# The second MLP's first layer in seven block products in place of eight

## The chip, the cores and the metric

The kernel runs on one core of a Trainium2 chip. The metric is the device time of one execution in microseconds (us); before the change the median of three runs is 594.81 us (594.66 to 596.38). The engines are named as the profile names them: PE (TensorE, the matrix multiplier), DVE (VectorE), ACT (ScalarE), POOL (GpSimd) and SP (which only issues DMAs here).

## The reference

A linear recurrence over 4 sequences of 768 tokens and 8 heads makes 3072 rows of 256 features, and two MLPs follow, each 256 to 2048 to 256:

```python
x = attn_out.transpose(0, 2, 1, 3).reshape(3072, 256)
x = softplus(x @ w_in1) @ w_out1
h = x @ w_in2                      # 256 -> 2048: what is changed
g = h * (1.0 / (1.0 + np.exp(-1.702 * h)))
out = g @ w_out2
```

## The kernel before, in words

Tokens are worked through in 6 chunks of 512 columns (`NC`, `TB`); features lie on the partitions. An MLP on one chunk is 16 tiles (`NF`), one for each 128 of the 2048 inner features; tile t runs from 0 to 191, 0 to 95 the first MLP and 96 to 191 the second. The recurrence is interleaved with the first MLP's first chunks. Chunk 5 (tiles 80 to 95) is the first MLP's last, chunk 6 (tiles 96 to 111) the second MLP's first.

An fp32 operand is held as a high half rounded to the matmul's format (fp32r) and a low half, the difference; one product is then three matmuls (high by high, high by low, low by high). For each tile, `g1` (L386) makes h with 6 matmuls (two contraction halves of 128 features, three each) in one of three PSUM banks `ps_h`. ACT applies the activation (L593) and rounds it to gh (`rnd`, L411), DVE makes the low half gl (`low`, L416), and two tiles later `g2` (L393) adds the tile into the output with 6 matmuls, three for each 128 output features j. `finish` (L421) copies a finished chunk's output from PSUM on ACT or DVE, and for the second MLP sends it to HBM from one of two buffers tagged "e". The MLPs' weights come as 64-bit floats in 16 units each, of 128 x 512 numbers; kind "2i" is the second MLP's first layer, "2o" its second. A unit is decoded by `w_scale` (L110, on DVE or ACT), `w_three` (L126, ACT), two dependent DVE instructions (`w_join_lo` and `w_join_sign`, L134 and L139), and is split by a rounding on ACT (L89) and a subtraction on POOL (`psub`, L82). The schedule is the program's order, written by hand, one in-order queue for each engine; an instruction that waits holds up all behind it on its engine. The decoding of the 16 units runs in half steps through chunk 5 (7 units) and chunk 6 (9 units), counted by `due`:

```python
            if c == NC - 1:
                due = 14 * (m + 1) // 16
            elif c == NC:
                due = min(2 * len(W2_units), 14 + 3 * (m + 1) // 2)
```

The first MLP's output stays in SBUF in the tensor `x2`; `x2split` splits one chunk of it ahead of that chunk's 16 tiles.

## Time and profile before

| | us |
|---|---|
| runs (median of 3) | 594.81 (594.66 to 596.38) |
| profiled execution, first to last instruction (span) | 591.5 |
| PE busy | 578.9 (98%) |
| DVE busy | 352.5 (60%) |
| ACT busy | 303.3 (51%) |
| POOL busy | 127.2 (21%) |

The profile is of one execution; of its own time it shows the span, and the runs' median lies 3.3 us above that. Busy times of one engine are sums of instruction times; a matmul's end is modelled, and matmuls overlap, so PE's rate is read from the distance of two starts. In a timeline row stand the start, the duration, the engine and line, output and inputs, and in brackets the idle time before it and what ended that.

### The profile page before, as it was taken

How to read it: one execution, taken by the hardware profiler on the slowest of the kernel's cores; microseconds unless marked ns; L12 is line 12 of the kernel's file. 1: busy time of each engine (PE TensorE's matmuls, PEld its weight loads, DVE VectorE, ACT ScalarE, POOL GpSimd, SP SyncE). 2: the span in 40 equal slices, each digit the busy share in tenths (PEclk: the TensorE clock that was granted, in tenths of full speed). 3: DMA queues.
4: the chain of work that ended last, by engine and by line, in shares of the span. 5: the costliest groups of instructions: out<-in, count | busy, mean ns of one | idle time of the engine just before them, and what ended most of it. 6: DMA issues, size and time to landing. Idle time of an engine off the chain costs nothing.

```text
span 591.5 us, 8905 instructions
## 1 busy us (share of the span) xinstructions
PE 578.9 (98%) x3452; PEld 462.7 (78%) x3452; DVE 352.5 (60%) x496; ACT 303.3 (51%) x518; POOL 127.2 (21%) x111
## 2 busy tenths in 40 slices
PE   6899999999999999999999999999999999999997
PEld 4555667888888888888888888888888888888886
DVE  5899969998787977975557684332332232232321
ACT  2656435544444444434577996454454554544443
POOL 1011336444364543540012333000000000000000
PEclk9799999999999999999999999999999999999999
DMA  8857741533414334240132430000000000000000
GB/s 270 297 178 239 257 161 48 158 104 132 154 68 161 109 131 129 89 164 2 38 106 72 117 133 1 35 2 0 37 0 1 36 1 0 37 0 2 35 2 35
DMA packets 26570, 52.32 MB, mean 88 GB/s; under 512 B 3072, under 2 KB 8608, under 8 KB 26528
## 3 DMA queue, kind: packets, MB, share of 16 engines
q1 hardware_dynamic: 26528, 51.75, 26.6%
q8 instruction: 27, 0.44, 0.3%
q14 instruction: 15, 0.12, 0.1%
HBM read 48.40 MB, written 3.34 MB: 87 GB/s over the span
## 4 chain that ended last, share of the span: by engine, by line
PE 90%; DVE 4%; DMA 3%; issue 1%; ACT 1%; SPq 0%; POOL 0%; DVEq 0%; POOLq 0%; ACTq 0%
PE h L391 42%; PE o L407 13%; PE o L409 13%; PE o L408 13%; PE o L405 3%; PE y L330 2%; PE cb L299 1%; DMA pq<-pack_q 1%; PE cb L275 1%; PE y L321 1%; DVE L L244 1%; DMA wraw_1o<-w1o 1%; DMA scr_z<-ac 1%; DVE L L309 1%; DVE gl L79 0%
## 5 line engine op out<-in xcount | busy, mean ns | idle before, releaser
L79 DVE TENSOR_TENSOR gl<-g,gh 128x512 fp32r<-128x512 f32 x176 | 140.4, 800 | 174.6 <-ACT gh L414 174.4
L593 ACT ACTIVATE g<-h 128x512 f32<-128x512 f32 x192 | 114.5, 596 | 240.6 <-PE h L391 230.1
L414 ACT ACTIVATE gh<-g 128x512 fp32r<-128x512 f32 x176 | 111.3, 632 | 5.6
L391 PE MATMUL h<-xh,w1ih 128*128 128x512 f32 x192 | 80.0, 417 | 0.5 <-ACT xh L357 0.5
L391 PE MATMUL h<-xl,w1ih 128*128 128x512 f32 x192 | 75.4, 393 | 0.9 <-DVE xl L79 0.9
L391 PE MATMUL h<-x2h,w2ih 128*128 128x512 f32 x192 | 74.7, 389 | 0.0
L391 PE MATMUL h<-x2l,w2ih 128*128 128x512 f32 x192 | 74.7, 389 | 0.0
L407 PE MATMUL o<-gh,w2ol 128*128 128x512 f32 x192 | 74.7, 389 | 0.0
L408 PE MATMUL o<-gh,w2oh 128*128 128x512 f32 x192 | 74.7, 389 | 0.0
L409 PE MATMUL o<-gl,w2oh 128*128 128x512 f32 x192 | 74.7, 389 | 0.0
L244 DVE TENSOR_TENSOR_SCAN L<-abz,eye 128x1024 f32<-128x1024 f32 (+1 forms) x25 | 63.4, 2534 | 3.4 <-PE abz L234 3.4
L407 PE MATMUL o<-gh,w1ol 128*128 128x512 f32 x160 | 63.1, 395 | 0.0
L409 PE MATMUL o<-gl,w1oh 128*128 128x512 f32 x160 | 62.3, 390 | 0.0
L408 PE MATMUL o<-gh,w1oh 128*128 128x512 f32 x160 | 62.3, 390 | 0.0
L391 PE MATMUL h<-xh,w1il 128*128 128x512 f32 x192 | 59.5, 391 | 1.4 <-DVE w1il L79 1.4
L391 PE MATMUL h<-x2h,w2il 128*128 128x512 f32 x192 | 59.1, 389 | 0.0
L82 POOL TENSOR_TENSOR rhs_bd<-tc,pk 64x512 fp32r<-64x512 f32 x32 | 53.4, 1669 | 1.2
L391 PEld LDWEIGHTS h<-xl,w1ih 128*128 128x128 f32 x192 | 36.1, 188 | 9.9 <-issue 2.6
L391 PEld LDWEIGHTS h<-xh,w1ih 128*128 128x128 f32 x192 | 36.1, 188 | 9.9 <-issue 2.2
L391 PEld LDWEIGHTS h<-xh,w1il 128*128 128x128 f32 x192 | 35.9, 188 | 10.0 <-DVE w1il L79 2.3
L409 PEld LDWEIGHTS o<-gl,w2oh 128*128 128x128 f32 x192 | 36.0, 188 | 7.5
L391 PEld LDWEIGHTS h<-x2h,w2il 128*128 128x128 f32 x192 | 36.0, 188 | 7.5
(102 smaller groups left out, 707.4 us busy)
## 6 DMA issues: line engine op xcount, KB each, us to landing
abz<-scr_z SPq DMA_DIRECT2D x22, 512.0 KB, 3.7
pk<-pack_s SPq DMA_DIRECT2D x16, 512.0 KB, 4.0
px<-pack_x SPq DMA_DIRECT2D x20, 320.0 KB, 3.0
wraw_1i<-w1i SPq DMA_DIRECT2D x8, 512.0 KB, 4.8
wraw_1o<-w1o SPq DMA_DIRECT2D x8, 512.0 KB, 4.3
wraw_2i<-w2i SPq DMA_DIRECT2D x8, 512.0 KB, 3.7
wraw_2o<-w2o SPq DMA_DIRECT2D x8, 512.0 KB, 3.6
out<-ot SPq DMA_DIRECT2D x12, 256.0 KB, 2.0
```

The lines of the kernel that those rows point to most:

```text
L79: nc.vector.tensor_sub(o, x, y)
L82: nc.gpsimd.tensor_tensor(out=o, in0=x, in1=y, op=ALU.subtract)
L244: nc.vector.tensor_tensor_scan(out=d["L"][:, h].rearrange("p h t -> p (h t)"), data0=d["abz"][:, h].rearrange("p h t -> p (h t)"), data1=e ...
L275: nc.tensor.matmul(d["cb", q // 2][:, q % 2, 0 : 2 * T], d["B"][r], d["C"][r], start=True, stop=True)
L330: nc.tensor.matmul(d["y"][32 * h : 32 * h + 32, g * T : g * T + T], d["x"][:, x0 : x0 + D], d["M", g][:, h, :], start=(s < NB), stop=True, ...
L391: nc.tensor.matmul(h, w[:, k, f], x[:, k, :], start=(n == 0), stop=(n == 5))
L405: nc.tensor.matmul(acc[c][j], plain[:, m, o], d["g"], start=first, stop=last)
L407: nc.tensor.matmul(acc[c][j], wl[:, m, o], d["gh"], start=first, stop=False)
L408: nc.tensor.matmul(acc[c][j], wh[:, m, o], d["gh"], start=False, stop=False)
L409: nc.tensor.matmul(acc[c][j], wh[:, m, o], d["gl"], start=False, stop=last)
L414: nc.scalar.activation(d["gh"], d["g"], AF.Copy)
L593: nc.scalar.activation(d["g"], d["h"], AF.Softplus if t < NT else AF.Gelu_apprx_sigmoid)
```

## The change

The 2048 inner features are taken in 8 weight units of 256 (unit q of kind "2i"), and chunks in 3 pairs p. For one unit and one pair, a group G (24 groups, G = 8p + q), there are four weight blocks a_fk of 128 x 128 (feature half f, contraction half k) and four input blocks b_kc (contraction half k, chunk c of the pair). Four tiles h(f, c) = a_f1 b_1c + a_f2 b_2c need eight block products; now seven are made, of three matmuls each:

- weights: s1 = a21 + a22, s2 = s1 - a11, s3 = a11 - a21, s4 = a12 - s2, made while a unit is decoded (four DVE instructions of 128 x 128, and seven blocks to split instead of four, so a "2i" unit has a second ACT rounding and a second POOL subtraction of 128 x 384);
- inputs: T1 = b12 - b11, T2 = b22 - T1, T3 = b22 - b12, T4 = b21 - T2 (`prep`, once for each pair: four DVE subtractions, and the split of seven blocks);
- products: P1 = a11 b11, P2 = a12 b21, P3 = s4 b22, P4 = a22 T4, P5 = s1 T1, P6 = s2 T2, P7 = s3 T3;
- sums: U1 = P1 + P6 and U2 = U1 + P7 (DVE, after ACT has copied P1 out of PSUM to `u_p`); h(0,0) = P1 + P2, where P2 is added in P1's bank; h(1,1) = U2 + P5; h(1,0) = U2 + P4; h(0,1) = U1 + P5 + P3, where P3 is added in P5's bank after DVE has read P5. So three of the four tiles pass through a DVE addition ahead of the activation.

In a group PE has 15 blocks of three matmuls: the seven products, and eight calls of `l2`, each three matmuls of the second layer for one tile and one j, taken from a queue (`queue`) that lags behind. Group 0 has 13 blocks, since two `l2` calls are left for the end. Decoding runs through chunk 5 (8 units, DVE's `w_scale`) and groups 0 to 5 (8 units, ACT's `w_scale`); `prep` for the first pair runs in chunk 5, for the second in groups 0 to 5, for the third in groups 8 to 13. Units 4 to 7 and the inputs of pairs 0 and 1 take the place of weights of the first MLP and of new buffers. The second MLP keeps two chunks' outputs open at a time; the last pair's four outputs are finished one behind the other at the end, the last two in the "e" buffers that the two ahead of them have just been sent from.

```diff
+BLOCK = {1: 0, 7: 1, 2: 2, 4: 3, 5: 4, 6: 5, 3: 6}
+BW = 7 * P
...
-        if kind[0] == "2" and q in (4, 6):
-
-            t = x2[:, 0, int(kind == "2o")]
+        if kind[0] == "2" and q >= 4 and (2 * q + int(kind == "2o")) % 3 == 0:
+            t = x2[:, 1, 1]
...
-        for t in range(2 * NT + 2):
...
+        def prep(p):
+            first, rest = home[p]
+            x0, x1 = x2[:, 2 * p], x2[:, 2 * p + 1]
+            t3 = hid.tile([P, TB], F32, tag="e", name=f"t3_{p}", bufs=2)
+            b11, b21, b12, b22 = x0[:, 0], x0[:, 1], x1[:, 0], x1[:, 1]
...
+            B1 = (first["h"], first["l"])
+            B22, T1, T2, T3, T4 = ((rest["h"][j], rest["l"][j]) for j in range(5))
+            xops[p] = {
+                1: tuple(v[:, 0] for v in B1), 2: tuple(v[:, 1] for v in B1),
+                3: B22, 4: T4, 5: T1, 6: T2, 7: T3,
+            }
+            high(B1, x0)
+            yield
+            vsub(t3, b22, b12)
+            yield
+            low_(B1, x0)
+            high(B22, b22)
+            yield
+            vsub(b12, b12, b11)
+            yield
+            low_(B22, b22)
+            high(T3, t3)
+            yield
+            vsub(b11, b22, b12)
+            yield
+            low_(T3, t3)
+            high(T1, b12)
+            yield
+            vsub(b21, b21, b11)
+            yield
+            low_(T1, b12)
+            high(T2, b11)
+            yield
+            low_(T2, b11)
+            high(T4, b21)
+            yield
+            low_(T4, b21)
+            yield
+        def unit_steps(u):
+            kind, q = W2_units[u]
+            t, lo = w_scale(kind, q, nc.vector if u < 8 else nc.scalar), w_three(kind, q)
+            yield
+            t = w_join(kind, q, t, lo)
+            if kind == "2i":
+                a11, a21, a12, a22 = (t[:, k, f * P : f * P + P] for k in range(2) for f in range(2))
+                s1, s2, s4 = (sums[0][:, i] for i in range(3))
+                nc.vector.tensor_add(s1, a21, a22)
+                vsub(a21, a11, a21)
+                vsub(s2, s1, a11)
+                vsub(s4, a12, s2)
+                parts = [
+                    (w2i["h"][q][:, 0 : 4 * P], w2i["l"][q][:, 0 : 4 * P], t.rearrange("p k f -> p (k f)")),
+                    (w2i["h"][q][:, 4 * P :], w2i["l"][q][:, 4 * P :], sums[0].rearrange("p s f -> p (s f)")),
+                ]
+            else:
+                parts = [(w2o["h", "unit"][q], w2o["l", "unit"][q], t)]
+            yield
+            for h, l, src in parts:
+                nc.scalar.activation(h, src, AF.Copy)
+            for h, l, src in parts:
+                psub(l, src, h.bitcast(F32))
+            if u + 3 < len(W2_units):
+                w_load(W_in[W2_units[u + 3][0]], *W2_units[u + 3])
+            yield
+        def decode(first, last):
+            us = {u: unit_steps(u) for u in range(first, last)}
+            next(us[first])
+            for u in range(first, last):
+                yield
+                next(us[u])
+                yield
+                if u + 1 < last:
+                    next(us[u + 1])
+                    yield
+                next(us[u])
+            yield
+        early = decode(0, 8)
...
+                    g, f, ct = (t - NT) // 4, (t - NT) // 2 % 2, t % 2
+                    d = tt[t]
+                    c, m = NC + 2 * (g // 8) + ct, 2 * (g % 8) + f
+                    a = acc_of(c, f"{c}")[j]
+                    o = slice(j * P, j * P + P)
+                    first = g % 8 == 0 and f == ct
+                    last = g % 8 == 7 and f != ct
+                    wh, wl = w2o["h"][m][:, o], w2o["l"][m][:, o]
+                    nc.tensor.matmul(a, wl, d["gh"], start=first, stop=False)
+                    nc.tensor.matmul(a, wh, d["gh"], start=False, stop=False)
+                    nc.tensor.matmul(a, wh, d["gl"], start=False, stop=last)
+                if last:
+                    finish(c, j)
...
+            u_p, u_1, u_2 = x2[:, 0, 0], x2[:, 0, 1], x2[:, 1, 0]
+            for G in range(24):
...
+                def bank(n):
+                    return ps_h.tile([P, TB], F32, tag="h", name=f"p{n}_{G}")
+                def product(n, dst, start=True):
+                    wh, wl = (w2i[x][q][:, BLOCK[n] * P : BLOCK[n] * P + P] for x in "hl")
+                    xh_, xl_ = xops[p][n]
+                    for i, (w, x) in enumerate(((wh, xh_), (wh, xl_), (wl, xh_))):
+                        nc.tensor.matmul(dst, w, x, start=start and i == 0, stop=i == 2, skip_group_check=not start)
+                def make(f, ct, src=None, add=None):
+                    d = tt[key(f, ct)] = {}
+                    d["g"] = hid.tile([P, TB], F32, tag="g", name=f"g{G}_{f}{ct}")
+                    if add is not None:
+                        nc.vector.tensor_add(d["g"], src, add)
+                        src = d["g"]
+                    nc.scalar.activation(d["g"], src, AF.Gelu_apprx_sigmoid)
+                    rnd(key(f, ct))
+                    queue.extend([(key(f, ct), 0), (key(f, ct), 1)])
+                b1 = bank(1)
+                product(1, b1)
+                nc.scalar.activation(u_p, b1, AF.Copy)
+                if lo12 is not None:
+                    low(lo12)
+                work(0)
+                l2()
+                b6 = bank(6)
+                product(6, b6)
+                nc.vector.tensor_add(u_1, b6, u_p)
+                l2()
+                product(2, b1, start=False)
+                make(0, 0, b1)
+                if G:
+                    l2()
+                b7 = bank(7)
+                product(7, b7)
+                nc.vector.tensor_add(u_2, b7, u_1)
+                low(key(0, 0))
+                work(0, 0, 1)
+                l2()
+                b5 = bank(5)
+                product(5, b5)
+                make(1, 1, b5, u_2)
+                if G:
+                    l2()
+                b4 = bank(4)
+                product(4, b4)
+                make(1, 0, b4, u_2)
+                low(key(1, 1))
+                l2()
+                product(3, b5, start=False)
+                make(0, 1, b5, u_1)
+                low(key(1, 0))
+                work(0, 1)
+                lo12 = key(0, 1)
+                l2()
+                l2()
+            low(lo12)
+            while queue:
+                l2()
...
-            elif t < 2 * NT:
-                g1(t, *w2[0:2], x2h[c - NC], x2l[c - NC])
...
+                second_open()
+                prep0 = prep(0)
-            due = 0
...
+                for _ in range(25 * (m + 1) // 16 - 25 * m // 16):
+                    next(early, None)
+                if m >= 4:
+                    next(prep0, None)
...
-            if m == 8 and NC - 1 <= c < 2 * NC - 1:
-                x2split(c - NC + 1)
+        catch_up(act_later)
+        catch_up(vec_later)
+        for _ in prep0:
+            pass
+        second()
```

On PE, for the second MLP before: one tile's first layer and a second layer's six (h is the tile's PSUM bank, o the output bank for j = 0 or 1, gh and gl the halves of g).

```order
L391 MATMUL h123_4045<-x2h1_3664,w2ih_3067 128x512
L391 MATMUL h123_4045<-x2l1_3665,w2ih_3067 128x512
L391 MATMUL h123_4045<-x2h1_3664,w2ih_3067 128x512
L391 MATMUL h123_4045<-x2l1_3665,w2ih_3067 128x512
L391 MATMUL h123_4045<-x2h1_3664,w2il_3068 128x512 x2
L407 MATMUL o112_0_3873<-gh121_4018,w2ol_3070 128x512
L408 MATMUL o112_0_3873<-gh121_4018,w2oh_3069 128x512
L409 MATMUL o112_0_3873<-gl121_4022,w2oh_3069 128x512
L407 MATMUL o112_1_3874<-gh121_4018,w2ol_3070 128x512
L408 MATMUL o112_1_3874<-gh121_4018,w2oh_3069 128x512
L409 MATMUL o112_1_3874<-gl121_4022,w2oh_3069 128x512
```

On PE now, the second half of group 2 (p5 and p4 are the banks of P5 and P4; xo holds the split T blocks; the gh and gl are of the tiles made a group earlier).

```order
L727 MATMUL p5_2_3734<-xo_3071,w2ih_3067 128x512 x2
L727 MATMUL p5_2_3734<-xo_3071,w2il_3069 128x512
L699 MATMUL o7_0_3592<-gh101_3666,w2ol_3070 128x512
L700 MATMUL o7_0_3592<-gh101_3666,w2oh_3068 128x512
L701 MATMUL o7_0_3592<-gl101_3688,w2oh_3068 128x512
L727 MATMUL p4_2_3746<-xo_3071,w2ih_3067 128x512 x2
L727 MATMUL p4_2_3746<-xo_3071,w2il_3069 128x512
L699 MATMUL o7_1_3593<-gh101_3666,w2ol_3070 128x512
L700 MATMUL o7_1_3593<-gh101_3666,w2oh_3068 128x512
L701 MATMUL o7_1_3593<-gl101_3688,w2oh_3068 128x512
L727 MATMUL p5_2_3734<-xo_3071,w2ih_3067 128x512 x2
L727 MATMUL p5_2_3734<-xo_3071,w2il_3069 128x512
```

A tile's 12 matmuls, 24 of 48 in the first layer for four tiles, have become blocks of three; the last two rows are P3, which writes the bank of P5 again and so comes after DVE's reading of it.

On DVE before, in chunk 6: the decoding of a "2i" and a "2o" unit between the low halves (wt is the unit, wraw its raw words).

```order
L134 SCALAR_TENSOR_TENSOR wt_2i5_3533<-wt_2i5_3533,wraw_2i5_3481 128x512
L139 SCALAR_TENSOR_TENSOR wt_2i5_3533<-wraw_2i5_3481,wt_2i5_3533 128x512
L79 TENSOR_TENSOR gl101_3589<-g101_3578,gh101_3580 128x512
L134 SCALAR_TENSOR_TENSOR wt_2o5_3561<-wt_2o5_3561,wraw_2o5_3509 128x512
L139 SCALAR_TENSOR_TENSOR wt_2o5_3561<-wraw_2o5_3509,wt_2o5_3561 128x512
L79 TENSOR_TENSOR gl102_3613<-g102_3604,gh102_3606 128x512
L134 SCALAR_TENSOR_TENSOR x2_97<-x2_97,wraw_2i6_3537 128x512
L139 SCALAR_TENSOR_TENSOR x2_97<-wraw_2i6_3537,x2_97 128x512
L79 TENSOR_TENSOR gl103_3640<-g103_3628,gh103_3630 128x512
```

On DVE now, all of group 2 (x2 holds u_p, U1 and U2 here, and the inputs of the pair that is prepared; g2_11 is h(1,1) of group 2; L733 are the additions with a PSUM operand).

```order
L748 TENSOR_TENSOR x2_97<-p6_2_3696,x2_97 128x512
L756 TENSOR_TENSOR x2_97<-p7_2_3714,x2_97 128x512
L82 TENSOR_TENSOR gl104_3719<-g2_00_3707,gh104_3709 128x512
L135 SCALAR_TENSOR_TENSOR wt_2o5_3690<-wt_2o5_3690,wraw_2o5_3572 128x512
L140 SCALAR_TENSOR_TENSOR wt_2o5_3690<-wraw_2o5_3572,wt_2o5_3690 128x512
L82 TENSOR_TENSOR w1ol_96<-x2_97,w1oh_95 128x512
L733 TENSOR_TENSOR g2_11_3738<-p5_2_3734,x2_97 128x512
L733 TENSOR_TENSOR g2_10_3750<-p4_2_3746,x2_97 128x512
L82 TENSOR_TENSOR gl107_3755<-g2_11_3738,gh107_3741 128x512
L733 TENSOR_TENSOR g2_01_3763<-p5_2_3734,x2_97 128x512
L82 TENSOR_TENSOR gl106_3768<-g2_10_3750,gh106_3753 128x512
L82 TENSOR_TENSOR x2_97<-x2_97 128x512
```

Four low halves for four tiles have become nine instructions (U1, U2, three additions and four low halves), and the "2o" unit's two and one low half of `prep` stand ahead of the addition for h(1,1), one subtraction of `prep` ahead of the last low half.

## Rows read from the trace of the kernel before

**Rows 1.** The page, parts 1 and 2: busy time, 40 slices.
```profile
span 591.5 us, 8905 instructions
...
PE 578.9 (98%) x3452; PEld 462.7 (78%) x3452; DVE 352.5 (60%) x496; ACT 303.3 (51%) x518; POOL 127.2 (21%) x111
...
PE   6899999999999999999999999999999999999997
...
PEclk9799999999999999999999999999999999999999
```

**Rows 2.** Busy time by stretch: chunk 5, chunk 6, the rest after it.
```profile
core 0: us, PE busy (x) PEld busy (x) DVE busy (x) ACT busy (x) POOL busy (x), PEclk, DMA share, GB/s
280.50:324.00 43.50, 43.50 (x194) 36.02 (x193) 26.89 (x40) 28.28 (x50) 7.74 (x6) 1.00 0.24 73
324.00:367.50 43.50, 43.50 (x193) 36.03 (x192) 29.38 (x38) 37.18 (x65) 14.38 (x10) 1.00 0.28 85
367.50:588.00 220.50, 220.49 (x973) 182.25 (x971) 63.86 (x94) 105.72 (x175) 0.00 (x0) 1.00 0.03 13
```

**Rows 3.** Timeline late in the second MLP: start, duration, instruction.
```profile
568.79 0.39 PE L391 MATMUL h<-x2h,w2ih 128*128 128x512 f32 x1
...
570.35 0.60 ACT L593 ACTIVATE g<-h 128x512 f32<-128x512 f32 x1 [1.46 <-PE h L391]
...
570.98 0.63 ACT L414 ACTIVATE gh<-g 128x512 fp32r<-128x512 f32 x1
...
571.51 0.39 PE L391 MATMUL h<-x2h,w2ih 128*128 128x512 f32 x1
...
571.64 0.69 DVE L79 TENSOR_TENSOR gl<-g,gh 128x512 fp32r<-128x512 f32 x1 [2.03 <-ACT gh L414]
```

**Rows 4.** Groups by line and shape, whole span: busy us, mean ns of one.
```profile
L79 DVE TENSOR_TENSOR xl<-y,xh 128x256 fp32r<-128x256 f32 x24 | 9.2, 416 | 2.8 <-ACT xh L357 2.8
...
L82 POOL TENSOR_TENSOR w2il<-wt_2i,w2ih 128x512 fp32r<-128x512 f32 x6 | 7.7, 1290 | 37.8 <-ACT w2ih L89 37.8
...
L129 ACT ACTIVATE wraw_2i<-wraw_2i 128x512 uint32<-128x512 uint8 x8 | 5.3, 665 | 0.0
...
L593 ACT ACT_TABLE_LOAD x1 | 1.3, 1283 | 0.0
```

**Rows 5.** Timeline of chunk 6, ACT, DVE and POOL.
```profile
327.13 0.62 ACT L89 ACTIVATE w2ih<-wt_2i 128x512 fp32r<-128x512 f32 x1
...
327.65 0.66 ACT L129 ACTIVATE wraw_2o<-wraw_2o 128x512 uint32<-128x512 uint8 x1
...
330.95 0.69 DVE L139 SCALAR_TENSOR_TENSOR wt_2o<-wraw_2o,wt_2o 128x512 uint32<-128x512 uint32 x1
...
331.56 0.69 DVE L79 TENSOR_TENSOR gl<-g,gh 128x512 fp32r<-128x512 f32 x1
...
333.36 1.37 POOL L82 TENSOR_TENSOR w2ol<-wt_2o,w2oh 128x512 fp32r<-128x512 f32 x1 [4.24 <-ACT w2oh L89]
333.50 1.78 DVE L79 TENSOR_TENSOR gl<-g,gh 128x512 fp32r<-128x512 f32 x1
```

**Rows 6.** Timeline in the first MLP: a DVE instruction with a PSUM operand.
```profile
223.77 0.69 DVE L309 TENSOR_TENSOR L<-cb,L 128x512 f32<-128x512 f32 x1 [0.83 <-PE cb L299]
...
223.82 1.29 POOL L82 TENSOR_TENSOR lb<-tb,pk 128x512 fp32r<-128x512 f32 x1 [2.29 <-PE cb L299]
```

**Rows 7.** Timeline early in the span: PE stopped by a late operand.
```profile
37.88 0.68 DVE L79 TENSOR_TENSOR w1il<-wt_1i,w1ih 128x512 fp32r<-128x512 f32 x1
...
38.62 0.73 PE L391 MATMUL h<-xh,w1il 128*128 128x512 f32 x2 [1.24 <-DVE w1il L79]
```

**Rows 8.** Timeline of the end, the last output copies and their DMAs.
```profile
587.35 1.28 ACT L427 ACTIVATE ot<-o 128x512 f32<-128x512 f32 x2 [2.14 <-PE o L409]
...
587.97 1.01 SPq L431 DMA_DIRECT2D out<-ot  x2
```

**Rows 9.** The page, part 6: us from issue to landing.
```profile
out<-ot SPq DMA_DIRECT2D x12, 256.0 KB, 2.0
```

More of the change, by code (lines that the diff above doesn't have):

```diff
@@ L400, in g2 @@
                 acc[c] = [ps_o.tile([P, TB], F32, tag=f"o{j}", name=f"o{t}_{j}") for j in range(2)]
-        first, last = m == 0, m == NF - 1
-        for j in range(2):
-            o = slice(j * P, j * P + P)
-            if plain is not None:
-                nc.tensor.matmul(acc[c][j], plain[:, m, o], d["g"], start=first, stop=last)
-                continue
-            nc.tensor.matmul(acc[c][j], wl[:, m, o], d["gh"], start=first, stop=False)
-            nc.tensor.matmul(acc[c][j], wh[:, m, o], d["gh"], start=False, stop=False)
-            nc.tensor.matmul(acc[c][j], wh[:, m, o], d["gl"], start=False, stop=last)
+        return acc[c]
+    def g2(t, j):
+        c, m = divmod(t, NF)
+        d = tt[t]
+        a = acc_of(c, t)[j]
+        first, last = m == 0, m == NF - 1
+        o = slice(j * P, j * P + P)
+        if t < NF:
+            nc.tensor.matmul(a, w1of[:, m, o], d["g"], start=first, stop=last)
+        else:
+            nc.tensor.matmul(a, w1ol[:, m, o], d["gh"], start=first, stop=False)
+            nc.tensor.matmul(a, w1oh[:, m, o], d["gh"], start=False, stop=False)
+            nc.tensor.matmul(a, w1oh[:, m, o], d["gl"], start=False, stop=last)
     def rnd(t):
@@ new lines, in decode, with second, l2, work @@
+        def decode(first, last):
[11 more added lines that the diff above has]
+        early = decode(0, 8)
+        def second():
+            for _ in early:
+                pass
+            second_home()
+            low(NT - 1)
+            units = decode(8, 16)
+            queue = [(NT - 2, 0), (NT - 2, 1), (NT - 1, 0), (NT - 1, 1)]
+            lo12 = None
+            def l2():
+                if not queue:
+                    return
+                t, j = queue.pop(0)
+                if t < NT:
+                    g2(t, j)
+                    c, m, last = NC - 1, t % NF, t % NF == NF - 1
+                else:
+                    g, f, ct = (t - NT) // 4, (t - NT) // 2 % 2, t % 2
+                    d = tt[t]
+                    c, m = NC + 2 * (g // 8) + ct, 2 * (g % 8) + f
+                    a = acc_of(c, f"{c}")[j]
+                    o = slice(j * P, j * P + P)
+                    first = g % 8 == 0 and f == ct
[8 more added lines that the diff above has]
+            for G in range(24):
+                p, q = divmod(G, 8)
+                if G == 0:
+                    back = [units, prep(1)]
+                elif G == 8:
+                    back = [units, prep(2)]
+                def work(*which):
+                    for i in which:
+                        next(back[i], None)
+                def key(f, ct):
+                    return NT + 4 * G + 2 * f + ct
+                def bank(n):
[55 more added lines that the diff above has]
+                l2()
@@ L561, in mixer_two_mlps @@
+        for t in range(NT):
             c, m = divmod(t, NF)
@@ L581, in mixer_two_mlps @@
                 at_pe(s, k)
-            if 2 <= t < NT + 2:
-                g2(t - 2, w1oh, w1ol, plain=w1of if t - 2 < NF else None)
-            elif t >= 2:
-                g2(t - 2, *w2[2:4])
+            if t >= 2:
+                for j in range(2):
+                    g2(t - 2, j)
             if mixing and late:
```

88 lines of the change are left out of this document (43 added, 45 removed).

## The prediction

> **What bounds the kernel now.** I read the page first: PE is busy 98% of a span of 591.5 us, at 9 tenths or more in 37 of 40 slices, with the granted clock at 9 tenths or more in all but the second [rows 1]. A busy PE need not be PE at its rate, so I looked at distances of starts next. Two first matmuls of neighbouring tiles start 571.51 - 568.79 = 2.72 us apart, for 12 matmuls: **0.2267 us for one matmul**, 0.68 us for three (a block) [rows 3]. The stretches agree: chunk 6 has 193 matmul records in 43.5 us, and PE idles in none of the three [rows 2]. So in the second MLP the number of matmuls sets the time, as long as the other engines keep up. Late in it they do so easily: DVE works 63.86 us of 220.5, ACT 105.72, POOL nothing. In chunks 5 and 6, where units are decoded, DVE has 26.89 and 29.38 us of 43.5, ACT 28.28 and 37.18, POOL 7.74 and 14.38 [rows 2]. The reader is to see that the change takes work from PE everywhere and lays work on DVE where DVE is fullest.
>
> **What it removes.** 24 groups x (48 - 45) = 72 matmuls x 0.2267 = **16.3 us**. This is firm: the 2.72 us hold six matmuls into an h bank and six into o banks, each change of bank included, so I see no price for changing it more often. Everything else is what of it comes back.
>
> **Prices.** A DVE instruction of 128 x 512 lasts 0.69 us; the next, if it needs nothing from it, starts 0.61 later (330.95 to 331.56) [rows 5], else about 0.72. On ACT the next starts 0.52 later (327.13 to 327.65) [rows 5], a rounding behind its activation 0.63 [rows 3]. POOL's subtraction takes 1.29 us [rows 4]; by width about 1.0 for 128 x 384. While POOL subtracts, a DVE instruction with two SBUF operands is held: one that began at 333.50, 0.14 us after POOL, lasted 1.78 in place of 0.69 and ended 0.55 after POOL [rows 5]. One with a PSUM operand is not held: it lasted 0.69 with POOL starting 0.05 us into it [rows 6]. So U1, U2 and the three new additions run beside POOL; low halves, joins, sums and `prep` don't. A 128 x 128 sum lies between 0.17 (a quarter of 0.69) and 0.42 (twice its width [rows 4]); I take 0.25, on the line between the two longer ones, so 1.0 for a unit's four. By the Trainium skill, VectorE: DVE Perf Modes, section The TRN2 errata, a two-input fp32 instruction lasts (columns + 151)/0.96 ns, 0.29 us here and 1.16 for four; the row of 512 columns agrees (0.69), and the sum would be 0.3 us longer by it.
>
> **A group without decoding.** Blocks of 0.68 us, P1 at 0: P2 is due at 2.72, P7 ends its data at 4.92 (7 blocks and the 0.16 by which a matmul outlasts its distance), P3 is due at 8.16. DVE: U2 at 4.96, low half of h(0,0) 5.57, h(1,1)'s addition 6.18 to 6.87, before P3 may overwrite its bank: **1.3 us to spare**. After P3 starts, DVE still has h(1,0)'s addition, a low half that waits for ACT, then h(0,1)'s addition, which ends 2.6 us after P3's start; ACT's activation and rounding follow (until 3.8), then the copy u_p (until 4.4), and P2 of the next group is due at 7 blocks, 4.76: **0.36 us to spare**. So groups 6 to 23 run at PE's rate. Pair 2's `prep` puts 0.6, once 1.2 us into the 1.3: it fits.
>
> **Groups 0 to 5, the term that decides.** What decoding and `prep` put ahead of h(1,1)'s addition, and ahead of u_p on ACT, comes off these two margins. A "2o" join is 1.33 on DVE, a "2i" join with sums 2.33, a `prep` step 0.6; a POOL subtraction that falls in holds DVE up to 1.2 more. On ACT a unit's roundings are 0.95 ("2i"), scale and three together 1.1 [rows 4, 5].
> - Group 2, by the order shown: join 1.33 + low half 0.6 = 1.94, less 1.3 = 0.65 late; ACT's two roundings of a "2i" unit end just as U2 runs, so both POOL subtractions (1.29 + 1.0) fall on the low half and the join: about 1.9 more. P3 waits **2.6**.
> - Group 0: join and sums 2.33; the ACT table load of 1.28 [rows 4] also lies ahead of h(0,0)'s activation, but the margin is like that above, as the group has 13 blocks: 1.6.
> - Group 1: P2 waits 1.2 (two roundings ahead of u_p, and the copy of chunk 5's output ahead of h(0,1)'s addition). P3 waits 2.0 (a 1024-column low half of 1.2 held by a POOL subtraction).
> - Group 3: P2 0.7 (scale and three ahead of u_p), P3 1.6 (2.33 + 0.6 - 1.3).
> - Group 4: P2 0.7, P3 1.4 (a held "2o" join makes U1 late, and a low half is held).
> - Group 5: P2 0.2, P3 2.7 (as group 2).
>
> Together **14.7 us**. Bounds: were no DVE instruction ever held, 8.1 is left (1.6, 1.2 + 0.8, 0.7, 0.7 + 1.6, 0.7, 0.2 + 0.6); were every subtraction to fall on waiting work, some 18.
>
> **Chunk 5.** DVE had 26.89 us there with six POOL subtractions, some 0.63 us of holding each, so 23.1 of its own. Added are one unit (scale and join, 1.7), four times 1.0 of sums, and `prep` (11 steps' worth of 0.61 less the 1.2 of the former split, 5.5): 34.3. POOL gets 8 x 1.29 + 4 x 1.0 = 14.4. If the two exclude each other that is 48.7 us of 43.5, 5.2 too much, and in-order waits for ACT waste some. A low half is ready about 3.6 us before its matmul now, which is used up first; but then it is missing at group 0, which starts with the tiles of the end of chunk 5. Bounds 0 and 6; I take **4**, near the upper, as the work exceeds the stretch.
>
> **Restart and end.** A stopped PE started 0.06 us after what it waited for, and its two matmuls took 0.73 in place of 0.61 [rows 7]: about 0.12 for each stop that the above doesn't have, x 16 stops = **2**. At the end, before, the last two copies follow one another, done at 588.63, and wait for matmuls alone [rows 8]. Now chunk 11's two output buffers are those of chunk 10, sent 1.36 us of matmuls earlier, and a DMA takes 2.0 [rows 9]: chunk 10's second copy is done 0.5 us before PE's end, its DMA lands 1.6 after it, and the last copy starts 1.7 after it, where it had only matmuls to wait for: **1.6** (bounds 0.5 and 2.5).
>
> **The sum.** Against the profiled execution: 591.5 - 16.3 + 14.7 + 4 + 2 + 1.6 = 597.5 of span; with the 3.3 us that the median of the runs lies above it, 600.8. Since each lateness is reckoned as if DVE could not catch up while PE stands, I round down: **600 us**, 0.9% slower.
>
> **The rivals.** A measurement of this kernel can tell about 0.3%, 1.8 us, from no change (593.0 to 596.6).
> - DVE and POOL miss each other. The place is groups 0 to 5: POOL's subtractions start when ACT's roundings end, and these may end while DVE makes PSUM additions or waits. For it: those additions are five of DVE's nine instructions and aren't held. Against: DVE has hardly a wait left in these groups. Price: 8.1 in the groups, 1 in chunk 5, 1 of restarts: 594.8 - 16.3 + 8.1 + 1 + 1 + 1.6 = 590.2. It decides the sign when all waits together stay under 12.9 (16.3 - 1.6 - 1.8). Chance 0.20.
> - Gain and loss cancel: waits of 12.9 to 16.5 us, 593.0 to 596.6, for instance 10.5 in the groups, 2.5 and 1.5. Chance 0.15.
> - The granted clock falls. In the second slice of the page PEclk is 7 tenths, where PE was still busy 8 tenths [rows 1]; in groups 0 to 5 PE would be busy about 60 us of 75. The price of half the clock for a quarter of the 60 us is 15 us: 615. Against: the waits are short (2.7 us at most) among matmuls of full size. The Trainium skill, TensorE: Matmul & The Clock Gate, section Why this matters for your kernels, warns that idle gaps between bursts of matmuls bring the lower clock back; no stretch of the second MLP shows it before. Chance 0.03.
>
> **Chances and range.** My forecast (waits above 16.5, full clock) has 0.62. Slower by over 0.3%: 0.62 + 0.03 = 0.65; within 0.3%: 0.15; faster: 0.20. Low bounds of all terms (8.1 + 0 + 1 + 0.5) give 588.1, high ones (18 + 6 + 3 + 2.5) 608.0; 8 in 10 I put between 591 and 606. The forecast's own range is 597 to 606.
>
> **What would show it.** In the profile after: matmul starts in groups 7 to 23 still 0.227 us apart and 10.2 us for a group, no waits of PE there; in the first six groups 70 to 76 us in place of 59.8, with PE waiting before P3 for DVE's addition of h(1,1) and before P2 for ACT's u_p; POOL subtractions above 1.29 and joins of 1.3 to 1.8 us; the last output copy starting over 1 us after the last matmul. Wrong would make me: a PE with no waits in chunk 5 and under 1 us a group in groups 0 to 5 (then 583 to 588), waits in the later groups, or a PEclk below 9 tenths after the first slices.

## The result and the profile after

The changed kernel takes **601.85 us** (median of four runs, 599.1 to 605.1) against 594.73 us of the kernel before in the same session: ratio 1.0114, 95% interval 1.0065 to 1.0163, slower by 1.1%. The forecast was 600.0, range 591 to 606. The profiled execution has a span of 599.2 us and a time of 601.0, 1.8 us more; in the other runs the two also lie 1.8 us apart. The 3.3 us that the prediction added to the span of before hold, besides these 1.8, another 1.5 by which that profiled execution lay below the median. All medians here are of executions at the usual granted clock (0.97 and more); one of e8_eight's twelve took 652.85 us at 0.854 and is left out.

The page of the changed kernel, parts 1 and 2, to be read beside [rows 1]:

```profile
span 599.2 us, 8999 instructions
...
PE 572.7 (96%) x3380; PEld 451.2 (75%) x3380; DVE 460.1 (77%) x667; ACT 325.3 (54%) x555; POOL 139.5 (23%) x119
...
PE   7999999999999999999989898879999999999996
...
DVE  5899969998787976974899897986676756665654
...
PEclk9699999999999999999999899999999999999999
```

PE has 72 instructions fewer (3452 to 3380) and is busy 6.2 us less, though its share fell from 98% to 96%: behind the first slice the tenths of 8 and 7 stand in slices 21 to 27, which are the end of chunk 5 and groups 0 to 5. DVE is busy 107.6 us more. Two things were not in [rows 1]: PE has gaps in these slices, and slice 23 shows a PEclk of 8.

What PE waits for, from the view of waits (engine, line and operand, the releaser; us in total, times, longest):

```profile
PE p L727 <- DVE g L733: 9.1, 5, 2.4
PE o L413 <- DVE gl L82: 3.6, 6, 0.9
...
PE p L727 <- ACT x L741: 0.9, 2, 0.5
```

L733 is `make`'s addition: all five waits are P3 for h(1,1)'s bank. The second line is late low halves of chunk 5 (five waits in chunk 5, one of 0.8 in group 0), the third is P2 for the copy u_p. The windows of the changed kernel by stretch show that nothing of this reaches the later groups, where PE is busy 174.00 of 174.00 us and DVE 111:

```profile
core 0: us, PE busy (x) PEld busy (x) DVE busy (x) ACT busy (x) POOL busy (x), PEclk, DMA share, GB/s
279.50:324.00 44.50, 42.31 (x182) 33.60 (x181) 37.13 (x54) 30.63 (x53) 13.71 (x9) 1.00 0.21 72
...
330.23:343.89 13.66, 11.00 (x40) 8.30 (x39) 11.66 (x20) 10.34 (x17) 1.91 (x2) 0.88 0.22 77
343.89:354.52 10.63, 10.58 (x46) 8.34 (x45) 9.56 (x13) 7.73 (x15) 5.04 (x3) 1.00 0.15 51
...
414.00:588.00 174.00, 174.00 (x769) 143.96 (x768) 111.26 (x169) 100.02 (x165) 0.00 (x0) 1.00 0.03 13
```

The second and third of these rows are groups 0 and 1. One P3 wait in full, group 2's, from the timeline (start, duration, engine, instruction):

```profile
359.99 1.29 POOL L85 TENSOR_TENSOR w1il<-wt_2i,w1ih 128x512 fp32r<-128x512 f32 x1 [7.18 <-ACT w1ih L652]
360.00 0.69 DVE L756 TENSOR_TENSOR x<-p,x 128x512 f32<-128x512 f32 x1
...
360.61 1.23 DVE L82 TENSOR_TENSOR gl<-g,gh 128x512 fp32r<-128x512 f32 x1
...
361.25 1.46 POOL L85 TENSOR_TENSOR w1il<-sums,w1ih 128x384 fp32r<-128x384 f32 x1
...
361.76 1.50 DVE L135 SCALAR_TENSOR_TENSOR wt_2o<-wt_2o,wraw_2o 128x512 uint32<-128x512 uint32 x1
...
363.29 0.69 DVE L140 SCALAR_TENSOR_TENSOR wt_2o<-wraw_2o,wt_2o 128x512 uint32<-128x512 uint32 x1
363.90 0.68 DVE L82 TENSOR_TENSOR w1ol<-x,w1oh 128x512 fp32r<-128x512 f32 x1
...
364.50 1.28 DVE L733 TENSOR_TENSOR g<-p,x 128x512 f32<-128x512 f32 x2
...
365.24 0.73 PE L727 MATMUL p<-xo,w2ih 128*128 128x512 f32 x2 [2.38 <-DVE g L733]
```

Read it by DVE. U2 reads PSUM and takes 0.69 beside POOL, as in [rows 6]. The low half of h(0,0), in SBUF alone, takes 1.23, the first half of the join 1.50: two POOL subtractions hold them. Behind the join stands a step of `prep`, and only then h(1,1)'s addition, whose product (P5) had been in its bank since 360.8. PE, out of second-layer blocks, stands for 2.38 us.

The end, to be read beside [rows 8]:

```profile
592.51 0.69 DVE L433 COPY ot<-o 128x512 f32<-128x512 f32 x1 [1.33 <-PE o L701]
...
593.44 0.39 PE L701 MATMUL o<-gl,w1oh 128*128 128x512 f32 x1
594.57 0.60 ACT L431 ACTIVATE ot<-o 128x512 f32<-128x512 f32 x1 [2.15 <-DMA out<-ot]
595.43 0.60 ACT L431 ACTIVATE ot<-o 128x512 f32<-128x512 f32 x1 [0.27 <-DMA out<-ot]
```

Both last copies wait for a DMA, not for PE.

**A yardstick for single profiles.** The runs of one kernel spread by about 1%, and part of that arises ahead of the second MLP: in the profiles of this study the token mixing's last row of 32 matmuls starts anywhere from 274.4 to 279.6 us. So I split each profile at points that all kernels share: the start of that row (M), the first matmul of chunk 6, which is group 0's P1 (S), the start of the last matmul (L) and the end (E).

```
us           M to S   S to L   L to E   M to E
before        48.76   263.61    3.9     316.3
after         53.25   263.21    5.8     322.3
difference    +4.5     -0.4    +1.9      +6.0
forecast      +4.7     -0.4    +1.6      +5.9
```

The forecast's row takes 4 us and six restarts of 0.12 for chunk 5, and -16.3 + 14.7 + 10 x 0.12 for the groups. The yardstick has a spread of its own: a second profile of the changed kernel (e10_after_again) has 53.25 again, but 265.08 from S to L, so the agreement to a tenth there is luck.

### The profile page after: what moved, and what is told of

It is laid out like the page before. It is cut to its first block, busy times and chain, and to the rows that moved or that the text cites. A ratio compares the mean times of both kernels' runs of the same rounds, so it can differ in the third digit from the quotient of the medians.

```text
span 599.2 us, 8999 instructions
## 1 busy us (share of the span) xinstructions
PE 572.7 (96%) x3380; PEld 451.2 (75%) x3380; DVE 460.1 (77%) x667; ACT 325.3 (54%) x555; POOL 139.5 (23%) x119
## 4 chain that ended last, share of the span: by engine, by line
PE 74%; DVE 18%; issue 3%; ACT 3%; DMA 1%; DVEq 0%; POOL 0%; ACTq 0%; POOLq 0%; SPq 0%
PE h L392 16%; PE p L727 15%; PE o L701 6%; PE o L699 6%; PE o L700 6%; PE o L411 5%; PE o L413 5%; PE o L412 5%; DVE gl L82 4%; PE o L409 3%; PE y L331 2%; PE cb L276 2%; DVE L L245 1%; PE cb L300 1%; DVE g L733 1%
## 5 line engine op out<-in xcount | busy, mean ns | idle before, releaser
L82 DVE TENSOR_TENSOR gl<-g,gh 128x512 fp32r<-128x512 f32 x176 | 146.4, 834 | 32.1 <-ACT gh L418 31.8
L809 ACT ACTIVATE g<-h 128x512 f32<-128x512 f32 x96 | 57.3, 596 | 123.6 <-PE h L392 113.3
L392 PE MATMUL h<-xh,w1ih 128*128 128x512 f32 x192 | 80.1, 417 | 0.5 <-ACT xh L358 0.5
L735 ACT ACTIVATE g<-g 128x512 f32<-128x512 f32 x72 | 45.3, 630 | 61.3 <-DVE g L733 59.9
L392 PE MATMUL h<-xl,w1ih 128*128 128x512 f32 x192 | 75.6, 394 | 1.0 <-DVE xl L82 1.0
L392 PE MATMUL h<-xh,w1il 128*128 128x512 f32 x192 | 59.6, 392 | 1.2 <-DVE w1il L82 1.2
L733 DVE TENSOR_TENSOR g<-p,x 128x512 f32<-128x512 f32 x72 | 48.9, 687 | 9.5 <-PE p L727 8.7
L756 DVE TENSOR_TENSOR x<-p,x 128x512 f32<-128x512 f32 x24 | 16.6, 692 | 38.0 <-PE p L727 37.6
L392 PEld LDWEIGHTS h<-xl,w1ih 128*128 128x128 f32 x192 | 36.1, 188 | 10.0 <-issue 2.6
L392 PEld LDWEIGHTS h<-xh,w1ih 128*128 128x128 f32 x192 | 36.1, 188 | 10.0 <-issue 2.4
L392 PEld LDWEIGHTS h<-xh,w1il 128*128 128x128 f32 x192 | 35.9, 188 | 9.9 <-DVE w1il L82 2.1
L310 DVE TENSOR_TENSOR L<-cb,L 128x512 f32<-128x512 f32 x40 | 27.0, 683 | 18.1 <-PE cb L300 17.3
L413 PEld LDWEIGHTS o<-gl,w1oh 128*128 128x128 f32 x160 | 30.0, 188 | 12.5 <-DVE gl L82 6.2
L699 PE MATMUL o<-gh,w2ol 128*128 128x512 f32 x96 | 37.9, 395 | 0.0
L700 PE MATMUL o<-gh,w2oh 128*128 128x512 f32 x96 | 37.9, 394 | 0.0
L701 PE MATMUL o<-gl,w2oh 128*128 128x512 f32 x96 | 37.8, 394 | 0.0
```

The source lines that it names most:

```text
L82: nc.vector.tensor_sub(o, x, y)
L392: nc.tensor.matmul(h, w[:, k, f], x[:, k, :], start=(n == 0), stop=(n == 5))
L413: nc.tensor.matmul(a, w1oh[:, m, o], d["gl"], start=False, stop=last)
L699: nc.tensor.matmul(a, wl, d["gh"], start=first, stop=False)
L700: nc.tensor.matmul(a, wh, d["gh"], start=False, stop=False)
L701: nc.tensor.matmul(a, wh, d["gl"], start=False, stop=last)
```

## The experiments

Ten runs, nine of kernels made from the changed one and one of the changed kernel again. Times are medians; ratios are to the kernel before, run on the same chip.

```
run               median us   ratio [95%]                M to S  S to L  L to E
e1_order            597.46    1.0036 [1.0009, 1.0062]     53.29  260.32   5.4
e2_nodecode         589.77    0.9913 [0.9880, 0.9946]     53.27  250.05   6.0
e3_dvesub           595.65    1.0039 [1.0009, 1.0069]     50.21  261.17   5.5
e4_fill             601.81    1.0122 [1.0085, 1.0158]     53.25  264.27   5.8
e5_slots            588.29    0.9882 [0.9844, 0.9920]     53.30  249.60   5.8
e6_slots_dve        583.16    0.9799 [0.9758, 0.9839]     50.22  248.60   5.5
e7_all              582.16    0.9780 [0.9744, 0.9816]     50.22  248.60   4.0
e8_eight            597.36    1.0029 [1.0001, 1.0056]     50.22  264.22   4.0
e9_rate             600.57    1.0082 [1.0048, 1.0117]     53.29  262.44   5.8
e10_after_again     602.75    1.0116 [1.0042, 1.0190]     53.25  265.07   5.8
```

The theory is that of the prediction: what stands ahead of h(1,1)'s addition on DVE, and ahead of u_p on ACT, stops PE. The main rivals: DVE is simply short of time in these groups, or the seven products stop PE by themselves.

**e1_order: the work behind the addition.**

```diff
                 low(key(0, 0))
-                work(0, 0, 1)
                 l2()
...
                 make(1, 1, b5, u_2)
+                work(0, 0, 1)
```

> The two steps of decoding and preparation between the low half of h(0,0) and the addition of h(1,1) are issued behind that addition; nothing else changes. Theory (PE stops before P3 because h(1,1)'s addition stands behind this work on DVE's queue): the waits before P3 in groups 0 to 5, 11.4 us in the changed kernel's trace with the clock's 1.7, shrink to under 4, while some wait comes back before P2 or before a gl, since DVE has as much to do as before: 595 to 597 us in place of 601.9. Rival (DVE is simply short of time in chunk 5 and groups 0 to 5, and the order only decides where PE stops): the stops move, their sum stays near 20 us, 600 to 603 us.

597.46 us. The waits of the reordered kernel:

```profile
PE p L727 <- ACT x L741: 7.8, 6, 2.0
PE o L413 <- DVE gl L82: 3.7, 6, 0.9
```

Not one wait before P3 is left, so it was this work that made them. But P2's wait for u_p went from 0.9 to 7.8, and S to L fell by 2.9 us only (4.8 against the second profile of the changed kernel). The timeline of the reordered kernel on ACT tells why u_p was late in group 3:

```profile
364.73 0.63 ACT L418 ACTIVATE gh<-g 128x512 fp32r<-128x512 f32 x1
365.26 0.66 ACT L121 ACTIVATE x<-wraw_2i 128x512 f32<-128x512 f32 x1
365.83 0.64 ACT L130 ACTIVATE wraw_2i<-wraw_2i 128x512 uint32<-128x512 uint8 x1
366.37 0.58 ACT L741 ACTIVATE x<-p 128x512 f32<-128x512 f32 x1
```

Group 2's h(1,0) and h(0,1) came late to ACT (their additions now stand behind the work), and the scale and three of the next unit stand between them and u_p. The lateness is handed on to the next in-order queue: theory and rival each hold by half.

**e2_nodecode: none of the work.**

```diff
-            units = decode(8, 16)
+            units = iter(())
...
-                    back = [units, prep(1)]
+                    xops[1] = xops[0]
+                    back = [units, iter(())]
...
-                    wh, wl = w2o["h"][m][:, o], w2o["l"][m][:, o]
+                    wh, wl = w2o["h"][m % 8][:, o], w2o["l"][m % 8][:, o]
```

(and `w2i[x][q % 4]` in `product`.)

> Left out: decoding of units 8 to 15 and the preparation of pair 1; the groups use units 0 to 3's blocks and pair 0's operands in their place, so matmuls, additions, activations and low halves are as many as before. Theory (all of the groups' stops come from decoding and preparation): groups 0 to 6 run at 10.2 us like the later ones, the 14.7 us of stops after chunk 5 go, 587 us; the stops of chunk 5 (5 us) and the last copies (1.8 us) stay. Rival (seven products into three banks with reads between them stop PE by themselves whenever it starts behind): 10.8 us or more in groups 0 to 5, 592 us or more.

589.77 us; M to S is unchanged, and S to L is 250.05 us. The 1092 matmuls from S to L (24 x 21 of the first layer, 24 x 24 + 12 of the second) have 1091 distances of 0.2267 us, 247.3 in all. Of the 2.7 us above that, 1.1 are the late low half of chunk 5 in group 0 and 1.4 a stop in group 12, where pair 2's preparation overwrites the operands that pair 1 shares here with pair 0: a thing of this edit. So no group stops by itself: the second rival is out. The median lies 2.8 us above the theory's 587, as M to E fell by 12.9 us and not by 14.7; the rest is inside the runs' spread.

**e3_dvesub: the subtractions on DVE.** Each unit's are collected and issued ahead of the next unit's join.

```diff
-                psub(l, src, h.bitcast(F32))
+                pending.append((l, src, h))
...
+            flush()
             t = w_join(kind, q, t, lo)
```

> The second MLP's weight subtractions run on DVE, each unit's ahead of the next unit's join, in place of POOL. Theory (holding by POOL is a large part of the lateness): in the stretch 280 to 414 us DVE's instructions with two SBUF operands are 19 us longer in sum than alone (42 low halves of 866 ns in place of 690 make 7.4 of it); these go, and 8 x (0.61 + 0.48) + 8 x 0.61 = 13.6 us of own work come: 5.7 us less on DVE, of which PE's stops give back most: 596 to 599 us. Rival (holding matters little, as DVE often waits anyway): DVE gets the 13.6 us on top where it is late, 604 to 610 us.

595.65 us, a little below the theory's 596 to 599: more instructions on DVE, and less time. Low halves in chunk 5 and the first groups, of the changed kernel (the view that groups instructions by form):

```profile
L82 DVE TENSOR_TENSOR gl<-g,gh 128x512 fp32r<-128x512 f32 x42 | 36.1, 866 | 10.8 <-ACT gh L418 10.8
...
L135 DVE SCALAR_TENSOR_TENSOR wt_2o<-wt_2o,wraw_2o 128x512 uint32<-128x512 uint32 x6 | 8.7, 1454 | 0.0
```

and with DVE's subtractions:

```profile
L82 DVE TENSOR_TENSOR gl<-g,gh 128x512 fp32r<-128x512 f32 x47 | 32.2, 687 | 12.5 <-ACT gh L418 12.5
...
L135 DVE SCALAR_TENSOR_TENSOR wt_2o<-wt_2o,wraw_2o 128x512 uint32<-128x512 uint32 x6 | 4.1, 684 | 0.0
```

866 ns became 687 and 1454 became 684. Chunk 5 got 3.0 us of its 4.5 back. The groups kept most of theirs (S to L 261.17): there the place of the work decides, held or not.

**e4_fill: matmuls into the wait.**

```diff
                 product(4, b4)
+                if G < 6:
+                    product(4, b4)
```

> P4 is computed twice in each of groups 0 to 5, into the same bank: 18 matmuls more, 4.1 us of PE's time, ahead of P3. Theory (there DVE sets the time and PE waits for it): the matmuls fall into the waits before P3, each of which shrinks by up to 0.68 us, and the time changes by under 1 us: 601 to 603 us. Rival (PE sets the time there, and the stops come with each product or bank change): the 4.1 us are added in full, 606 us.

601.81 us, ratio 1.0122 beside the changed kernel's 1.0114. S to L, 264.27 us, lies between the changed kernel's two profiles (263.21 and 265.08), each of which has a fall of the clock in it, as told below; this one has none. So the groups where the second has none tell most: groups 0, 1, 4 and 5 take 12.11, 13.25, 12.14 and 13.13 us here, 12.13, 13.22, 12.12 and 13.10 there. P3's waits of that second profile and of this kernel:

```profile
PE p L727 <- DVE g L733: 10.3, 6, 2.4
```

```profile
PE p L727 <- DVE g L733: 6.2, 5, 1.7
```

They are shorter by the 4.1 us that the added matmuls last. In groups 0 to 5 the number of matmuls doesn't set the time.

**e5_slots: the same work in other places.** One unit in each of groups 0 to 7; the low half of h(0,0) and all of the work now stand behind the additions that PE waits for.

```diff
+                unit = unit_steps(8 + G) if G < 8 else iter(())
...
                 nc.scalar.activation(u_p, b1, AF.Copy)
-                if lo12 is not None:
-                    low(lo12)
-                work(0)
+                next(unit, None)
...
                 nc.vector.tensor_add(u_1, b6, u_p)
+                next(unit, None)
...
                 make(0, 0, b1)
+                next(unit, None)
...
-                low(key(0, 0))
-                work(0, 0, 1)
...
                 make(1, 1, b5, u_2)
+                low(key(0, 0))
...
                 low(key(1, 0))
-                work(0, 1)
+                step()
                 l2()
                 l2()
+                low(key(0, 1))
+                step()
```

The three calls of `unit` are scale and three, join, and roundings with subtractions; `step` is one step of `prep`, in groups 1 to 6.

> Units 8 to 15 are decoded one in each of groups 0 to 7: scale behind u_p on ACT, join between U1 and U2 on DVE, roundings behind h(0,0)'s activation; the low half of h(0,0) stands behind h(1,1)'s addition, and pair 1's preparation takes two steps at the end of each of groups 1 to 6. The work is the same. Theory (the groups' stops come from what stands ahead of h(1,1)'s addition on DVE and ahead of u_p on ACT, and neither engine is short of time): the 14.7 us of stops in groups 0 to 6 fall below 3, the 5 us of chunk 5 stay: 590 us in place of 601.9. Rival (DVE is short of time there, 11 us of work in 10.2 us of a group where POOL holds it): the stops only move as in the first experiment, 597 us.

588.29 us; S to L is 249.60, 0.4 below that of the kernel without the work (whose stop in group 12 this one doesn't have). Group 2 from the timeline of the kernel with slots, DVE and POOL:

```profile
358.96 0.68 DVE L757 TENSOR_TENSOR x<-p,x 128x512 f32<-128x512 f32 x1
359.75 0.69 DVE L734 TENSOR_TENSOR g<-p,x 128x512 f32<-128x512 f32 x1
360.36 0.74 DVE L82 TENSOR_TENSOR gl<-g,gh 128x512 fp32r<-128x512 f32 x1
361.02 0.68 DVE L734 TENSOR_TENSOR g<-p,x 128x512 f32<-128x512 f32 x1
361.81 0.72 DVE L82 TENSOR_TENSOR gl<-g,gh 128x512 fp32r<-128x512 f32 x1
```

```profile
359.26 1.29 POOL L85 TENSOR_TENSOR w1il<-wt_2i,w1ih 128x512 fp32r<-128x512 f32 x1 [9.44 <-ACT w1ih L652]
360.51 1.47 POOL L85 TENSOR_TENSOR w1il<-sums,w1ih 128x384 fp32r<-128x384 f32 x1
```

h(1,1)'s addition follows U2 at once, and POOL's two subtractions now run beside additions from PSUM; the low halves between them take 0.74 and 0.72. DVE is not short of time in the groups: the first rival is out too.

**e9_rate: the slots' spread, the old places.** Work per group as in e5_slots, but the low half of h(0,0), the join and a step of `prep` stand again ahead of h(1,1)'s addition, and the low half of h(0,1) again behind the next group's u_p. Against e5_slots:

```diff
                 nc.scalar.activation(u_p, b1, AF.Copy)
+                if lo12 is not None:
+                    low(lo12)
                 next(unit, None)
...
                 nc.vector.tensor_add(u_1, b6, u_p)
-                next(unit, None)
...
                 make(0, 0, b1)
-                next(unit, None)
...
+                low(key(0, 0))
+                next(unit, None)
+                step()
                 l2()
...
+                next(unit, None)
                 make(1, 1, b5, u_2)
-                low(key(0, 0))
...
                 step()
+                lo12 = key(0, 1)
                 l2()
                 l2()
-                low(key(0, 1))
-                step()
```

> As the slots experiment, with the same work in each group (one unit in each of groups 0 to 7, two steps of preparation in each of groups 1 to 6), but the join and one step of preparation stand between the low half of h(0,0) and h(1,1)'s addition, where the changed kernel has such work, and the roundings behind them. It tells whether the slots experiment won by the places or by spreading the work thinner. Theory (places): P3 waits for the join and the step less the margin of 1.3 us, 1.6 us in groups 2, 4 and 6, 1.0 in group 0, 0.6 in groups 1, 3 and 5, and 0.12 for each restart: 7.3 us more from group 0's P1 to the last matmul than the slots experiment's 249.6 us. Rival (thinner work is enough): under 2 us more, 250 to 252 us.

600.57 us, S to L 262.44, 12.8 us above e5_slots (expected 7.3; some 1.6 us of the difference are a fall of the granted clock, below). The waits of this kernel before P3 are back:

```profile
PE p L729 <- DVE g L735: 8.7, 6, 2.3
```

The changed kernel's two profiles have 263.21 and 265.08. So spreading the work thinner gave little; the places gave most.

**e6_slots_dve and e7_all: chunk 5 and the end.** e6_slots_dve puts the subtractions of units 0 to 7 on DVE as in e3_dvesub; e7_all also gives the last chunk's outputs another tag:

```diff
+                if u < 8:
+                    pending.append((l, src, h))
+                else:
+                    psub(l, src, h.bitcast(F32))
...
-            o = hid.tile([P, TB], F32, tag="e", name=f"ot{c}_{j}", bufs=2)
+            o = hid.tile([P, TB], F32, tag="g" if c == 2 * NC - 1 else "e", name=f"ot{c}_{j}", bufs=3 if c == 2 * NC - 1 else 2)
```

> As the slots experiment, and units 0 to 7 have their subtractions on DVE, each ahead of the next join; units 8 to 15 keep theirs on POOL. Theory: chunk 5 loses its holds as in the experiment with all subtractions on DVE, where its stops were 1.7 us in place of 5.1: 3.5 us below the slots experiment, 586.5 us. Rival (chunk 5 then hands its lateness to group 0): no faster than the slots experiment, 590 us.

> As the one with slots and DVE's subtractions, and the last chunk's two output copies write buffers of the tag g in place of those that chunk 10's copies fill. Theory (the last copies wait for chunk 10's DMAs): the last copy starts under 1 us after the last matmul, and the time is 1.6 us below that experiment, 585 us. Rival (the last output's own DMA sets the end anyway): no difference.

583.16 and 582.16 us. M to S fell by 3.1 us in both. The gain of the tag is inside the runs' spread, but the profile shows it: L to E fell from 5.5 to 4.0. The last two copies in e6_slots_dve start 1.1 and 2.0 us behind the start of the last matmul, 578.39:

```profile
579.52 0.60 ACT L431 ACTIVATE ot<-o 128x512 f32<-128x512 f32 x1 [2.15 <-DMA out<-ot]
580.38 0.60 ACT L431 ACTIVATE ot<-o 128x512 f32<-128x512 f32 x1 [0.27 <-DMA out<-ot]
```

and in e7_all both wait for PE alone, and are done (575.53 + 1.28) 1.0 behind it:

```profile
575.53 1.28 ACT L431 ACTIVATE ot<-o 128x512 f32<-128x512 f32 x2 [0.76 <-PE o L712]
...
575.79 0.39 PE L712 MATMUL o<-gl,w1oh 128*128 128x512 f32 x1
```

e7_all is the best kernel here, 2.2% (1.8 to 2.6) below the kernel before.

**e8_eight: eight products again, on e7_all.** P4 is computed twice in every group.

> As the one with all three edits, and P4 is computed twice in each of the 24 groups: eight products a group, as many matmuls as before the change. Theory (groups run at 0.2267 us a matmul when nothing is late): 72 x 0.2267 = 16.3 us above the experiment with all three edits, less what is left of stops there: 600 to 601 us. Rival (the time of seven products is set by DVE or by the changes of bank, not by matmuls): under 10 us above it.

597.36 us; S to L is 15.62 us above e7_all, of 16.3. Its groups are 0.68 us longer, but for groups 0, 1 and 9, which are 0.28, 0.32 and 0.10 less than that: e7_all has small stops there, which this kernel mostly lacks. Where nothing is late, a matmul is worth its 0.2267 us.

**e10_after_again: the changed kernel once more.**

> The changed kernel once more, for the clock and the place of the spread of its times. If the granted clock's fall behind group 0's wait before P3 belongs to this kernel, it is there again and group 0 takes over 12.5 us; if it came by chance, group 0 takes 12 us. If the spread of the runs arises ahead of the second MLP, the time from the last matmul of token mixing to the end is again 322.2 us within 0.3, whatever the span is.

602.75 us. Group 0 takes 12.13 us, so the clock's fall there doesn't come each time. The other half of my expectation failed: M to S is 53.25 again, but M to E is 324.1. The granted clock fell here too, in group 2 and not in group 0:

```profile
366.00:367.00 1.00, 1.00 (x4) 0.81 (x3) 0.82 (x2) 0.97 (x3) 0.00 (x0) 0.50 0.69 264
367.00:368.00 1.00, 1.00 (x4) 0.71 (x4) 1.00 (x3) 0.82 (x2) 0.00 (x0) 0.50 0.00 0
```

Groups 0 and 1 together took 25.35 us, in the first profile 24.29, although there the fall made group 0 1.5 us longer (13.66 to 12.13). Counted from S, DVE's instructions start at the same times in both profiles, to 0.02 us, up to 20.2 us: what PE lost by the clock was time that it would have waited. Then two instructions change places. In the second profile POOL's subtraction starts first, and DVE's low half of 1024 columns is held:

```profile
348.70 1.55 POOL L85 TENSOR_TENSOR w1ol<-x,w1oh 128x512 fp32r<-128x512 f32 x1 [2.14 <-ACT w1oh L652]
...
349.02 2.31 DVE L82 TENSOR_TENSOR x2l<-x,x2h 128x1024 fp32r<-128x1024 f32 x1
```

In the first DVE starts first, by 0.04 us, and POOL is held:

```profile
350.45 1.22 DVE L82 TENSOR_TENSOR x2l<-x,x2h 128x1024 fp32r<-128x1024 f32 x1
350.49 2.32 POOL L85 TENSOR_TENSOR w1ol<-x,w1oh 128x512 fp32r<-128x512 f32 x1 [2.50 <-ACT w1oh L652]
```

The low half stands ahead of h(1,1)'s addition, so group 1's P3 waits 1.2 us in the second profile and 0.05 in the first. The fall in group 2 made that group 0.9 us longer (13.83 to 12.89), of which group 3 gave back 0.1.

## Why the prediction was right

- **What is removed, 16.3 us.** Confirmed by e8_eight against e7_all (15.62, and 0.7 of stops that vanish) and by the later groups at PE's rate.
- **Groups 0 to 5, 14.7 us (bounds 8.1 to 18).** Right in mechanism; that the size agreed so well is in part luck. The six groups took 75.5 us, in the second profile 77.4 (forecast 70 to 76), and S to L changed by -0.4 and by +1.5 (forecast -0.4). The waits before P3 and P2, by their matmuls' starts, sum to 11.4 us, in the second profile to 12.9: the term was 3.3 or 1.8 us too large. Two things that the sum didn't have, and small gaps, made up for it: the fall of the clock (some 1.6 us of matmul time in each profile) and the late low half of chunk 5 in group 0 (1.1). Group 0 (1.6 forecast, 1.9 waited), group 3 (0.7 and 1.6; 0.5 and 1.8) and group 5 (2.7; 2.4) came near to what was worked out. So did group 2 (2.6; 2.4), but of other parts: POOL made the low half and the join 1.4 us longer in place of 1.9, and U2 started 5.48 us behind P1 in place of 4.96, as U1 ahead of it was late. Group 1's 1.2 and 2.0 were nearly absent in the first profile, and 0.9 and 1.2 in the second: the held low half that the prediction names there came or not as POOL or DVE started first (e10_after_again). Group 4's were 0.3 and 0.7 of 0.7 and 1.4; no run singles out why.
- **Chunk 5, 4 us and restarts.** 4.5 measured, 4.7 forecast. The cause given, DVE and POOL excluding each other, is shown for 3.0 us, which came back without POOL's subtractions (e3_dvesub, e6_slots_dve); the other 1.5 stayed.
- **The end, 1.6 us.** +1.9 from the last matmul to the end, and 1.5 gone with another buffer (e7_all).
- **The price of a 128 x 128 sum, 0.25.** Four took 1.06 us by their starts in e5_slots (357.90 to 358.96), each 0.28 to 0.29 long. The estimate by the Trainium skill, VectorE: DVE Perf Modes, section The TRN2 errata, was 0.29 for one: the trace agrees on the duration, while the next starts sooner.
- **The clock, chance 0.03.** It fell, but for 3.4 us and some 1.6 us of matmul time, not for the 15 that the rival priced. The PEclk of 8 in slice 23 is one of the signs that the prediction named as showing it wrong; it is this one fall, and none of the other signs came. The changed kernel, by the windows of one us behind the P3 of group 0:

```profile
341.00:342.00 1.00, 1.00 (x4) 0.80 (x3) 0.55 (x1) 0.97 (x3) 0.00 (x0) 0.50 0.02 4
342.00:343.00 1.00, 1.00 (x3) 0.78 (x3) 1.00 (x3) 0.60 (x1) 0.00 (x0) 0.50 0.00 0
```

- **Span and median.** The span was 599.2 where 597.5 was forecast, as M lies 1.75 us later than in the profile of before, ahead of anything that was changed. The 3.3 us from span to median were 2.6 in the changed kernel (601.85 less 599.2): 1.8 from span to time as in every run, and 0.8, in place of 1.5, by which the profiled execution lay below the median. Together they make the 1.05 us by which 601.85 lies above the sum's 600.8; the rounding down to 600 went the wrong way.

The prediction took the places of the work as given, and there the price was right; that the same work in other places costs almost nothing (249.6 of 247.3 us) it didn't say.

## What to carry to other kernels

Fewer matmuls pay only where PE sets the time. When a change lays work on another engine, list for each wait of PE what stands ahead of its releaser on that in-order queue, and move all that PE doesn't wait for behind it, on every queue at once: moved on DVE alone (e1_order) the lateness went to ACT, moved on both (e5_slots) it was gone with the same work. POOL's work with SBUF operands belongs beside DVE's additions from PSUM, or on DVE itself. And a control that puts the removed matmuls back (e4_fill, e8_eight) tells at once whether PE is the bound. One profile is not enough where two engines hold each other: in group 1 here 0.04 us between two starts decided on 1.1 us.
